# ScalarE takes a quarter of the first one-hot squares, all last stores leave from its queue, and a half tile of values is copied last

## The chip, the cores and the metric

The kernel runs on one core of one Trainium2 chip. A core has a matrix engine (TensorE, PE in the profile, with its weight loads shown as PEld), three engines for elementwise work (VectorE = DVE, ScalarE = ACT, GpSimd = POOL), a small engine that mostly issues transfers (SyncE = SP) and 16 DMA engines. Each engine works through its own list of instructions in order; they wait for each other with semaphores. The metric is the time of one execution on the device in microseconds (us), the median of several.

## The reference

Four batches of 1088 tokens go through an attention with polynomial features, and the result through a layer of 8 experts of which each token uses two.

```python
def phi(x):                       # x: (4, 4 heads, 1088, 32)
    a = np.einsum('rd,bhsd->bhsr', S1, x)
    b = np.einsum('rd,bhsd->bhsr', S2, x)
    return np.einsum('bhsi,bhsj->bhsij', a, b).reshape(*x.shape[:-1], r * r)
q_p, k_p = (phi(q), phi(k))
kv = np.einsum('bhsf,bhsd->bhfd', k_p, v)
z = np.sum(k_p, axis=2)
num = np.einsum('bhsf,bhfd->bhsd', q_p, kv)
den = np.einsum('bhsf,bhf->bhs', q_p, z)[..., None] + 1e-06
attn_out = (num / den).astype(np.float32)
x = np.ascontiguousarray(attn_out.transpose(0, 2, 1, 3)).reshape(B * S, H * D)   # (4352, 128)
...
logits = x @ w_gate
noise_scale = np.log1p(np.exp(x @ w_noise))
noisy_logits = logits + noise_scale * noise
top2 = np.argpartition(-noisy_logits, 2, axis=1)[:, :2]
top2_l = np.take_along_axis(noisy_logits, top2, axis=1)
top2_l = top2_l - top2_l.max(-1, keepdims=True)
top2_w = np.exp(top2_l)
top2_w /= top2_w.sum(-1, keepdims=True) + 1e-09
for e in range(E):
    for k in range(2):
        mask = top2[:, k] == e
        h = np.maximum(x[mask] @ w1[e], 0.0)   # 128 -> 1024
        out[mask] += top2_w[mask, k, None] * (h @ w2[e])
```

## The kernel before

**Stages.** The attention is done batch by batch (features L606 to L628, keys times values L669, queries L717 and L728). Then comes the routing of the tokens in steps `w`: router 0 takes the first four tiles of 128 tokens of the first batch, router 1 the other five of it, routers 2 to 4 the other batches. A router takes the logits, the two largest (L896 to L912), the mask `mk` of the chosen experts (L925, L927), counts by matmuls with triangles and ones how many tokens before a token chose the same expert (`counts`, L934 and L937), and from that a row in the memory `xs`, sorted by experts (L965 to L976). The gate weights `g` go through ScalarE (L906), GpSimd (L942), VectorE (L944) and GpSimd again (L945). The tokens times their weight (`xg`, L986) are scattered to `xs` by GpSimd's indirect DMAs, one for each tile and choice (L809).

**Blocks.** The experts work on blocks `u` of 128 or 256 rows of `xs`: fetch `xb`, turn it to `bT`, first matmuls to `hp` (L1094), relu to `h` on ScalarE (L1102), second matmuls to `acc` (L1109), copy to `y`, scatter to `pairs` (L809). Between these, TensorE does the attention of the next batch.

**The first four blocks** (`u < DIRECT = 4`) don't wait for scattered rows. For each of the four token tiles `c` a one-hot square `o` is made (L1040): row place against the token's position `pos`, times its gate `gm`. A matmul of the tokens with the square (`turn`, L1046) picks and turns the rows at once. `place` is a constant 128x128 tile; `pos` is made at L955 from the counts, `gm` at L961. VectorE makes these squares, except for the fourth of block 0, which GpSimd makes.

**Who sets the order.** Nothing of the order is written by hand. Every step is added as a `Job` with the engine, an estimated cost, what it reads and writes, and a priority (a lower number goes first). `Plan.order` is a list scheduler: at each step it takes those that could start within 0.3 us of the earliest, and of them the one of the lowest priority. For a TensorE job behind ScalarE's or VectorE's work it adds a margin `SLACK` = 0.5 us to the time at which the input is expected, once the plan is past 30 us (L105). For transfers, `margin` adds to the expected landing. The resulting lists are written once, so each number shifts places in all five lists. Where TensorE would idle in the plan before 28 us, it is given dummy matmuls on `zb` (L1421).

**The head's values.** The first batch's values come in as four full pieces and two small ones (`load_v`, L362). Copies make them to `vaug`: four full head copies and one for the half tile (L645), which stand with equal priority.

**The end.** Results are gathered from `pairs` (`pr`, issued by SyncE), added in twos (L1165), for the last batch's late pieces added to what TensorE computed (`bank`, L1172), and stored. `sums` (L1148) cycles through the queues it is given; the last call gives ("ACT", "SP", "SP") for the three pieces: the first store is issued by ScalarE, the others by SyncE. Then every engine loads `flag` (L1426) and branches past a fallback that serves an overflow of the blocks (L1428); SyncE waits for all transfers, and the engines close together (L1456).

Of the kernel before, what the change touches and what calls it, by code (L numbers as in the profile page):

```python
# [12 lines left out]
AF = mybir.ActivationFunctionType  # L13
# [16 lines left out]
class Job:  # L30
    def __init__(self, engines, cost, emit, lat, prio, size):
        self.engines, self.cost, self.emit, self.lat, self.prio, self.size = engines, cost, emit, lat, prio, size
        self.far, self.margin = False, 0.0
        self.paced = 0.0
        self.deps, self.opens, self.end, self.done = set(), [], None, None


class Plan:
# [17 lines left out]
    def new(self, tag):  # L56
        return Buf(tag)
# [30 lines left out]
    def order(self):  # L88
        free, done, moved, paced, lanes = {}, [], 0.0, [], []
        left = {j: len(j.deps) for j in self.jobs}  # L90
        after = {j: [] for j in self.jobs}
        for j in self.jobs:
            for d in j.deps:
                after[d].append(j)
        cand = [j for j in self.jobs if not left[j]]
        number = {j: i for i, j in enumerate(self.jobs)}

        def ready(j, e):

            at = 0.0  # L100
            for d in j.deps:
                if d.engine == e and d.size is None and not d.far:
                    at = max(at, d.end)
                elif e == "PE" and d.engine in ("ACT", "DVE") and d.done > self.HEAD:
                    at = max(at, d.done + self.SLACK)  # L105
                else:
                    at = max(at, d.done)
            return at

        while cand:  # L110
            starts = []
            for j in cand:
                at = 0.0
                for b in j.opens:
                    bufs, _, used = self.tags[b.tag]
                    if b.placed or len(used) < bufs:
                        continue
                    ends = [x.done for x in used[-bufs].users]
                    if None in ends:
                        at = None  # L120
                        break
                    at = max(at, max(ends))
                if at is None:
                    continue
                if j.size is not None:
                    if "SP" in j.engines:
                        at = max(at, moved - self.AHEAD)
                    if "POOL" not in j.engines and len(lanes) >= self.LANES:
                        at = max(at, lanes[-self.LANES])
                if j.paced and paced:  # L130
                    at = max(at, paced[-1] + j.paced)
                for e in j.engines:
                    starts.append((max(at, free.get(e, 0.0), ready(j, e)), j, e))
            assert starts, [(j.engines, j.prio, [b.tag for b in j.opens]) for j in cand]
            first = min(x[0] for x in starts)
            _, s, _, j, e = min((j.prio, s, number[j], j, e) for s, j, e in starts if s <= first + self.SOON)
            cand.remove(j)
            cost = j.cost[e] if isinstance(j.cost, dict) else j.cost
            j.start, j.end, j.engine = s, s + cost, e
            free[e] = j.end  # L140
            if j.paced:
                paced.append(s)
            j.done = j.end + j.lat + self.SYNC
            if j.size is not None:
                moved = max(moved, j.end + 0.6) + j.size / self.RATE
                j.done = max(j.done, moved + 0.8 if e == "SP" else j.end + 1.4 + 2 * j.size / self.RATE)
                if e != "POOL":
                    lanes.append(j.done)
                j.done += j.margin
            j.opens = [b for b in j.opens if not b.placed]  # L150
            for b in j.opens:
                b.placed = True
                self.tags[b.tag][2].append(b)
            done.append(j)
            for a in after[j]:
                left[a] -= 1
                if not left[a]:
                    cand.append(a)
        assert len(done) == len(self.jobs)
        return done  # L160
# [14 lines left out]
def kernel(  # L175
# [57 lines left out]
    def add(engines, cost, emit, **kw):  # L233

        if hold and engines in ("DVE", "PE"):
            kw["after"] = tuple(kw.get("after", ())) + tuple(hold)
        elif hold and engines == EV:
            engines = "ACT"
        return plan.add(engines, cost, emit, **kw)
# [3 lines left out]
    def tag(name, bufs, shape, dtype=F32, space=pool):  # L243
        plan.tag(name, bufs, lambda: space.tile(list(shape), dtype, name=name, tag=name, bufs=bufs))
# [48 lines left out]
    def vec(n):  # L293
        return 0.155 + 0.00104 * n

    def act(n):
        return 0.155 + 0.00086 * n
# [64 lines left out]
    def load_v(b, prio, queues=("SP",)):  # L362
        t = new("vld")
        vlds[b] = t
        src = v[b].rearrange("h (t n) d -> t h n d", n=TN)
        for l in range(4):
            dma(queues[l % len(queues)], lambda l=l: t.t[32 * l:32 * l + 32, :, 0:C, :].rearrange("p h c d -> p h (c d)"),
                lambda l=l: src[:, :, C * l:C * l + C, :].rearrange("t h c d -> t h (c d)"),
                (), [(t, l)], prio, size=131e3, issue=1.2, margin=MARGIN if b > 1 else 8.0 if b else VLATE)
        for l in range(2):  # L370
            dma(queues[l % len(queues)], lambda l=l: t.t[32 * l:32 * l + 32, :, C, :], lambda l=l: src[:, :, 32 + l, :],
                (), [(t, 4 + l)], prio, size=16e3, issue=0.6, margin=MARGIN if b > 1 else 8.0 if b else 0.0)

    w1s = const.tile([P, E, F], F32, name="w1s")
    w2s = const.tile([P, E, FJ, D], F32, name="w2s")
# [263 lines left out]
    def keys_values(b, prio, head=False, after=(), early=None):  # L639
        kT, qT, pk, pq, va = new("kT"), new("qT"), new("phk"), new("phq"), new("vaug")  # L640
        kld, qld, vld = klds[b], qlds[b], vlds[b]
        for h in range(H):
            add(("ACT", "POOL") if head else "ACT", {"ACT": act(256), "POOL": 0.4} if head else act(256), lambda e, h=h: copy(e, va.t[:, 0:C, h, 0:DH], vld.t[:, h, 0:C, :]),
                r=["ones_v"] + [(vld, l) for l in range(4)], w=[(va, h)], prio=prio + 2.2, after=hold)
        add("ACT", act(128), lambda e: A.copy(va.t[0:HB, C, :, 0:DH], vld.t[0:HB, :, C, :]),  # L645
            r=["ones_v", (vld, 4), (vld, 5)], w=[(va, H)], prio=prio + 2.2, after=hold)
        for i, (c0, c1) in enumerate(((0, 2), (2, 6), (6, 8)) if head else ((0, 4), (4, 8))):
            if early is not None and i == 0:
                turned(kT, kld, c0, c1, 22, True)
# [166 lines left out]
    def router(b, t0, n, w, x, lg, prio):  # L816
# [13 lines left out]
        def dve(cost, emit, r, w_, p=0, after=()):  # L830
            def step(e):
                ins = emit()
                if w == 0 and ins is not None:
                    marks.append((plan.now.end, ins))
            return add("DVE", cost, step, r=[B_.get(k, k) if isinstance(k, str) else k for k in r],
                w=[B_.get(k, k) if isinstance(k, str) else k for k in w_], prio=prio + p, after=after)
# [95 lines left out]
        def counts(e):  # L932
# [3 lines left out]
            for s in range(1, n + 1):  # L936
                T.matmul(ps.t[:, E * s:E * (n + 1)], lhsT=ones[:],  # L937
                         rhs=mk[:, 0:n + 1 - s, :].rearrange("p i e -> p (i e)"), start=False, stop=(s == n),
                         skip_group_check=True)
        add("PE", 0.06 * (n + 1), counts, lat=0.15, r=[B_["mk"], "earlier", "ones"], w=[ps], prio=prio)  # L940

        add("POOL", 0.25, lambda e: G.tensor_scalar(out=g1(), in0=g2(), scalar1=1.0, scalar2=1e-9, op0=ALU.add, op1=ALU.add),  # L942
            r=[(B_["g"], 1)], w=[(B_["g"], 0)], prio=prio - 0.5)
# [7 lines left out]
        if w == 0:  # L951

            pos, gm = new("pos"), new("gm")
            onehot.update(pos=pos, gm=gm, x=x)
            dve(q1, lambda: V.scalar_tensor_tensor(out=pos.t[:], in0=ps3()[:, 0:n, :], scalar=1.0, in1=t3("mk"),  # L955
                                                   op0=ALU.add, op1=ALU.mult), [ps, "mk"], [pos], -0.5)

            def gates():
                V.tensor_tensor(out=B_["f2"].t[:, :, 0:n, :], in0=B_["first"].t[:, :, 0:n, :],
                                in1=B_["g"].t[:, :, 0:n].unsqueeze(3).to_broadcast([P, 2, n, E]), op=ALU.mult)  # L960
                V.tensor_add(out=gm.t[:], in0=B_["f2"].t[:, 0, 0:n, :], in1=B_["f2"].t[:, 1, 0:n, :])  # L961
            dve(2 * q1, gates, ["first", "g"], ["f2", gm])

        def rows_of():
            V.tensor_tensor(out=t3("row"), in0=ps3()[:, 0:n, :], in1=pl.unsqueeze(1).to_broadcast([P, n, E]), op=ALU.add)  # L965
# [56 lines left out]

    tag("pos", 1, [P, 4, E])
    tag("gm", 1, [P, 4, E])


    TOP = -1000
# [2 lines left out]
    def block(u, w, e, r, n):  # L1030
# [5 lines left out]
        if u < DIRECT:  # L1036
            oh = new("o")
            for c in range(4):
                add(("POOL" if u == 0 and c == 3 else "DVE"), 0.85 if u == 0 and c == 3 else vec(64), lambda e_, c=c: (
                    G if e_ == "POOL" else V).tensor_scalar(  # L1040
                    out=oh.t[:, c, :], in0=place[:], scalar1=onehot["pos"].t[:, c, e:e + 1],
                    scalar2=onehot["gm"].t[:, c, e:e + 1], op0=ALU.is_equal, op1=ALU.mult),
                    r=["place", onehot["pos"], onehot["gm"]], w=[(oh, c)], prio=-900 if u == 0 else 12.5 + u)

            for c in range(4):
                gather = add("PE", mm(P), lambda _, c=c: T.matmul(  # L1046
# [353 lines left out]
        if w == 4:  # L1400
            sums(B - 1, part_of(B - 1, [(0, 4)]), w, 901)
    pieces = part_of(B - 1, [(4, 2), (6, 2)], True)
    sums(B - 1, [pieces[0], pieces[2], pieces[1]], NW, 902, ("ACT", "SP", "SP"))

    def idle(a, b):

# [54 lines left out]
```

## Time and profile before

| | us |
|---|---|
| median of 3 runs | 350.83 (350.19 to 351.37) |
| the profiled execution | 352.57 |
| its span in the profile | 350.6 |
| TensorE's clock in it | 0.993 of full |

Busy time of each engine in stretches of the span:

| stretch, us | PE | DVE | ACT | POOL |
|---|---|---|---|---|
| 0 to 25 | 22.81 | 18.75 | 9.01 | 18.14 |
| 25 to 34 | 8.15 | 8.32 | 2.66 | 6.15 |
| 34 to 82 | 46.46 | 34.43 | 20.60 | 36.90 |
| 82 to 134 | 51.11 | 32.99 | 19.62 | 41.34 |
| 134 to 343 | 208.65 | 52.55 | 81.02 | 131.79 |
| 343 to 350.5 | 0.06 | 0.42 | 0.00 | 0.00 |

In the profile a line of the timeline gives the start in us from the start of the span, the duration in us, the engine, the line of the kernel, the operation, output<-input by the program's names with shapes, how many instructions were merged (x4), and in brackets how long the engine was idle before and what it then waited for. An engine name with a q (SPq) stands for its sequencer: issues of transfers, semaphores, branches. The list of waits has the total in us, the number of times and the longest.

### The profile page before, as it was taken

Reading aid. Unit: us, or ns where it says so; the run is one execution under the profiler, and the core shown is the slowest. Engines: PE = TensorE matmul, PEld = TensorE weight load, DVE = VectorE, ACT = ScalarE, POOL = GpSimd, SP = SyncE. Lnnn points to the kernel's source line nnn. Section 1 sums busy time; section 2 is a strip of 40 time slices with the busy share of each in tenths; the row PEclk is TensorE's granted clock in tenths of the full one; section 3 lists DMA queues with packets and bytes.
Section 4 is the critical chain, followed back from the end, with each engine's and each line's share of the span. In section 5 each row is a group of like instructions: output and inputs, shape, how many; then the busy total and the mean of one; then the engine's idle time right before and its main releaser. Section 6 shows DMA issues by size and latency. Waiting matters only on the chain.

```text
span 350.6 us, 7490 instructions
## 1 busy us (share of the span) xinstructions
PE 337.2 (96%) x2586; PEld 314.1 (90%) x2586; DVE 147.5 (42%) x550; ACT 132.9 (38%) x297; POOL 234.3 (67%) x385
## 2 busy tenths in 40 slices
PE   8999999998999999999999999999999999999991
PEld 3858999998999988999999999999999999999990
DVE  6789894867536669556760001011101010212111
ACT  2343643442533344413434333433343334434330
POOL 8856759895999863988898988978334433454310
PEclk9999999999999999999999999999999999999997
DMA  7999849135571386411533213454126211115421
GB/s 201 351 348 258 267 121 310 40 77 147 133 215 40 70 188 126 121 47 31 93 60 70 60 40 60 78 178 104 39 36 185 63 32 29 26 32 177 134 71 39
DMA packets 68922, 41.17 MB, mean 117 GB/s; under 512 B 49877, under 2 KB 61078, under 8 KB 68880
## 3 DMA queue, kind: packets, MB, share of 16 engines
q1 hardware_dynamic: 63584, 31.09, 35.7%
q0 software_dynamic: 4704, 9.15, 7.9%
q10 hardware_dynamic: 592, 0.41, 0.5%
q8 instruction: 21, 0.34, 0.4%
q14 instruction: 21, 0.17, 0.2%
HBM read 24.18 MB, written 16.65 MB: 116 GB/s over the span
## 4 chain that ended last, share of the span: by engine, by line
PE 84%; DVE 5%; DMA 4%; POOL 2%; issue 1%; SPq 1%; ACT 1%; POOLq 0%; DVEq 0%
PE acc L1109 34%; PE hp L1094 33%; PE bank L606 4%; PE bank L728 4%; PE bank L669 4%; DMA kq<-in_k_dram 2%; PE bank L717 2%; POOL pairs L809 1%; DMA xb<-xs 1%; PE turn L1046 1%; PE bank L1241 1%; SPq L338 1%; DVE kT L590 1%; POOL zb L808 0%; DMA ix<-xs 0%
## 5 line engine op out<-in xcount | busy, mean ns | idle before, releaser
L1109 PEld LDWEIGHTS acc<-w2s,h 128*128 128x128 f32 x1152 | 146.0, 192 | 5.1 <-ACT h L1102 0.4
L1109 PE MATMUL acc<-w2s,h 128*128 128x128 f32 x1152 | 150.4, 275 | 0.0
L1094 PE MATMUL hp<-bT,w1s 128*128 128x128 f32 (+1 forms) x768 | 148.2, 328 | 0.2 <-ACT h L1102 0.2
L1102 ACT ACTIVATE h<-hp 128x512 f32<-128x512 f32 x144 | 85.9, 597 | 126.1 <-PE hp L1094 125.9
L1094 PEld LDWEIGHTS hp<-bT,w1s 128*128 128x128 f32 x768 | 111.7, 191 | 6.2 <-ACT h L1102 0.7
L809 POOL DMA_INDIRECT pairs<-y,ix x66 | 65.8, 997 | 64.2 <-ACT y L322 52.8
L809 POOL DMA_INDIRECT xs<-xg,to x72 | 74.3, 1031 | 20.2 <-issue 9.6
L808 POOL MEMSET zb<- 128x400 bf16 (+1 forms) x142 | 63.1, 444 | 0.2
L1082 DVE STREAM_TRANSPOSE bT<-xb 128x256 f32<-128x256 f32 (+1 forms) x40 | 15.6, 390 | 111.6 <-PE hp L1094 99.7
L322 ACT COPY y<-acc 128x128 f32<-128x128 f32 (+1 forms) x48 | 15.3, 319 | 27.2 <-PE acc L1109 24.7
L1165 DVE TENSOR_TENSOR o<-pr 128x512 f32<-128x512 f32 (+2 forms) x13 | 6.7, 525 | 37.5 <-DMA pr<-pairs 37.5
L728 PE MATMUL bank<-kvw,pT 128*128 128x98 f32 x144 | 18.2, 274 | 0.0
L728 PEld LDWEIGHTS bank<-kvw,pT 128*128 128x128 f32 x144 | 17.3, 192 | 0.5 <-DVE kvw L322 0.3
L669 PE MATMUL bank<-phk,vaug 128*128 128x128 f32 (+1 forms) x108 | 13.1, 277 | 0.0
L322 ACT COPY lo<-bank 128x256 f32<-128x256 f32 (+3 forms) x20 | 6.6, 328 | 16.8 <-PE bank L606 14.0
L669 PEld LDWEIGHTS bank<-phk,vaug 128*128 128x128 f32 (+1 forms) x108 | 12.5, 191 | 0.4
L322 ACT COPY pT<-bank 128x512 f32<-128x512 f32 (+1 forms) x16 | 8.8, 560 | 10.0 <-PE bank L717 8.0
L628 DVE TENSOR_TENSOR phk<-ab 128x512 f32<-128x512 f32 (+1 forms) x20 | 12.2, 631 | 0.4
L614 DVE TENSOR_TENSOR ab<-bank,lo 128x256 f32<-128x256 f32 (+3 forms) x20 | 7.2, 361 | 12.3 <-ACT lo L322 12.0
L628 DVE TENSOR_TENSOR phq<-ab 128x512 f32<-128x512 f32 (+1 forms) x20 | 11.9, 629 | 0.2
L986 DVE TENSOR_TENSOR xg<-x,g 128x512 f32<-128x512 f32 (+1 forms) x16 | 11.2, 748 | 0.0
L1421 PE MATMUL hp<-zb 128*128 128x512 bf16 x30 | 9.3, 442 | 1.7 <-DVE zb L439 1.3
(175 smaller groups left out, 240.6 us busy)
## 6 DMA issues: line engine op xcount, KB each, us to landing
xs<-pad SPq DMA_DIRECT2D x9, 516.0 KB
w1s<-in_moe_w_dram SPq DMA_DIRECT2D x8, 512.0 KB
w2s<-in_moe_w_dram SPq DMA_DIRECT2D x8, 512.0 KB
pr<-pairs SPq DMA_DIRECT2D x7, 512.0 KB
xb<-xs SPq DMA_DIRECT2D x96, 32.0 KB
kq<-in_k_dram SPq DMA_DIRECT2D x4, 544.0 KB
kq<-in_q_dram SPq DMA_DIRECT2D x4, 544.0 KB
vld<-in_v_dram SPq DMA_DIRECT2D x14, 128.0 KB
```

The lines of the kernel that those rows point to most:

```text
L322: paces.append(A.copy(o, i) if e == "ACT" else V.tensor_copy(o, i))
L606: T.matmul(ps.t[rows, 2 * W * i:2 * W * i + 2 * W], lhsT=lhsT, rhs=sk[:].rearrange("p c h x -> p (c h x)"), start=True, stop=True)
L628: V.tensor_tensor(out=jobs[i][2].t[rows, jobs[i][1]:jobs[m - 1][1] + 1, :, :].rearrange("p c h (i j) -> p (c h) i j", i=R), in0=factors(i, ...
L669: T.matmul(kvp.t[:, P * a:P * a + P], lhsT=va.t[0:K, t, hs, :].rearrange("p h d -> p (h d)"), rhs=pk.t[0:K, t, hs, :].rearrange("p h f -> ...
L728: T.matmul(ps2.t[:, c0:c0 + 2 * YW], lhsT=pT.t[:, P * (2 * i + a):P * (2 * i + a) + P], rhs=kvw.t[:, a, :], start=True, stop=True)
L808: G.memset(zb[:, 0:FIRST_SPACER if kind == "first" else SPACER], 0.0)
L809: ins = G.indirect_dma_start(**kw)
L986: V.tensor_tensor(out=xg.t[:, i, c0:c1, 0:D], in0=x.t[:, c0:c1, :], in1=B_["g"].t[:, i, c0:c1].unsqueeze(2).to_broadcast([P, c1 - c0, D]), ...
L1082: add("DVE", vec(P * n), lambda _: V.transpose(bT.t[:, 0:P * n], flat()), r=[xb], w=[bT], prio=TOP + u)
L1094: T.matmul(hp.t[:, P * n * i:P * n * (i + 1)], lhsT=w1s[:, e, P * (js * g + i):P * (js * g + i + 1)], rhs=bT.t[:, 0:P * n], start=True, st ...
L1102: paces.append(A.activation(out=h.t[:], in_=hp.t[:], func=AF.Relu))
L1109: T.matmul(acc.t[:, D * c:D * c + D], lhsT=h.t[:, P * (n * i + c):P * (n * i + c + 1)], rhs=w2s[:, e, j, :], start=(j == 0 and c == 0), st ...
```

## The change

Four things change; the rest of the file stays, and below L1040 lines stand 14 lower in the new file.

1. The square of tile `c = 3` of each of the first four blocks is made by ScalarE in two steps: the absolute value of `pos` minus `place`, then relu of `gm` minus `gm` times that. It is `gm` where place and position agree and 0 elsewhere, since both are whole numbers and `gm` is not negative. The negative of `gm` for that tile is a new tile `less`, made by GpSimd. The other three squares are VectorE's in all four blocks. The squares' priorities are now (-900, 12.9, 14.5, 15.5), where they were -900 and 12.5 + u.
2. The counts of routers 1 to 4 get a planning margin of 1.0 in place of 0.5.
3. The small transfers of the first values get a planning margin, and the copy of the half tile the priority 2.9 in place of 2.2 in the head.
4. The last three stores are all issued by ScalarE.

```diff
@@ class Job
-        self.far, self.margin = False, 0.0
+        self.far, self.margin, self.slack = False, 0.0, None
@@ Plan.order, ready
-                    at = max(at, d.done + self.SLACK)
+                    at = max(at, d.done + (self.SLACK if j.slack is None else j.slack))
@@ load_v
-                (), [(t, 4 + l)], prio, size=16e3, issue=0.6, margin=MARGIN if b > 1 else 8.0 if b else 0.0)
+                (), [(t, 4 + l)], prio, size=16e3, issue=0.6, margin=MARGIN if b > 1 else 8.0 if b else VLATE + 0.5)
@@ keys_values
-            r=["ones_v", (vld, 4), (vld, 5)], w=[(va, H)], prio=prio + 2.2, after=hold)
+            r=["ones_v", (vld, 4), (vld, 5)], w=[(va, H)], prio=prio + (2.9 if head else 2.2), after=hold)
@@ the router
-        add("PE", 0.06 * (n + 1), counts, lat=0.15, r=[B_["mk"], "earlier", "ones"], w=[ps], prio=prio)
+        counted = add("PE", 0.06 * (n + 1), counts, lat=0.15, r=[B_["mk"], "earlier", "ones"], w=[ps], prio=prio)
+        counted.slack = None if w == 0 else 1.0
...
+            less = new("less")
+            onehot["less"] = less
+            add("POOL", 0.25, lambda e: G.tensor_scalar(out=less.t[:], in0=gm.t[:, 3, :], scalar1=-1.0, scalar2=None, op0=ALU.mult),
+                r=[gm], w=[less], prio=prio - 0.5)
@@ block
-                add(("POOL" if u == 0 and c == 3 else "DVE"), 0.85 if u == 0 and c == 3 else vec(64), lambda e_, c=c: (
-                    G if e_ == "POOL" else V).tensor_scalar(
+                if c == 3:
+
+                    add("ACT", act(P), lambda e_, c=c: A.activation(
+                        out=oh.t[:, c, :], in_=place[:], func=AF.Abs, scale=-1.0, bias=onehot["pos"].t[:, c, e:e + 1]),
+                        r=["place", onehot["pos"]], w=[(oh, c)], prio=(-900, 12.9, 14.5, 15.5)[u])
+                    add("ACT", act(P), lambda e_, c=c: A.activation(
+                        out=oh.t[:, c, :], in_=oh.t[:, c, :], func=AF.Relu, scale=onehot["less"].t[:, e:e + 1],
+                        bias=onehot["gm"].t[:, c, e:e + 1]), r=[onehot["gm"], onehot["less"]], w=[(oh, c)], prio=(-900, 12.9, 14.5, 15.5)[u])
+                    continue
+                add("DVE", vec(P), lambda e_, c=c: V.tensor_scalar(
                     out=oh.t[:, c, :], in0=place[:], scalar1=onehot["pos"].t[:, c, e:e + 1],
                     scalar2=onehot["gm"].t[:, c, e:e + 1], op0=ALU.is_equal, op1=ALU.mult),
-                    r=["place", onehot["pos"], onehot["gm"]], w=[(oh, c)], prio=-900 if u == 0 else 12.5 + u)
+                    r=["place", onehot["pos"], onehot["gm"]], w=[(oh, c)], prio=(-900, 12.9, 14.5, 15.5)[u])
@@ the last call of sums
-    sums(B - 1, [pieces[0], pieces[2], pieces[1]], NW, 902, ("ACT", "SP", "SP"))
+    sums(B - 1, [pieces[0], pieces[2], pieces[1]], NW, 902, ("ACT",))
```

More of the change, by code (lines that the diff above doesn't have):

```diff
@@ L1024 @@
     tag("gm", 1, [P, 4, E])
+    tag("less", 1, [P, E])
     TOP = -1000
```

## The prediction, made before the changed kernel ran

> **What bounds the kernel now.** I read the page's busy shares first, then its slices, then the waits, the timeline at each remaining gap of TensorE (PE), and last what follows its last matmul.
>
> ```profile
> PE 337.2 (96%) x2586; PEld 314.1 (90%) x2586; DVE 147.5 (42%) x550; ACT 132.9 (38%) x297; POOL 234.3 (67%) x385
> PE   8999999998999999999999999999999999999991
> ```
>
> PE is the bound at full clock, so a change can win only where PE is idle or after it has ended. The stages show where: PE is busy 8.15 of 9.00 us in 25 to 34, 46.46 of 48 in 34 to 82, 51.11 of 52 in 82 to 134 and 208.65 of 209 in 134 to 343; then come 7.5 us without PE. So some 3.3 us of gaps lie between 25 and 134, nothing after, and 7.5 us at the end.
>
> The head (timeline 25 to 28), where the first block's four one-hot squares are made:
>
> ```profile
> 25.06 1.30 DVE L1040 TENSOR_SCALAR o<-place,pos,gm 128x128 f32<-128x128 f32 x3
> 25.13 0.87 POOL L1040 TENSOR_SCALAR o<-place,pos,gm 128x128 f32<-128x128 f32 x1 [0.80 <-DVE pos L955]
> ...
> 26.50 0.68 PE L1046 MATMUL turn<-o,x 128*128 128x128 f32 x4 [0.18 <-DVE row L965]
> ...
> 27.54 1.86 PEld L1094 LDWEIGHTS hp<-bT,w1s 128*128 128x128 f32 x16 [0.23 <-ACT bT L322]
> ```
>
> Third router (w=2): GpSimd (POOL) issues back to back until its gate step, VectorE (DVE) goes on from that, and PE's counts come last. The three groups are POOL's, DVE's and PE's timeline:
>
> ```profile
> 77.92 0.97 POOL L809 DMA_INDIRECT pairs<-y,ix  x1 [0.17 <-issue]
> 78.96 0.27 POOL L942 TENSOR_SCALAR g<-g 128x9 f32<-128x9 f32 x1
> ```
> ```profile
> 79.27 0.21 DVE L944 RECIPROCAL g<-g 128x9 f32<-128x9 f32 x1 [0.64 <-POOL g L942]
> 79.40 0.25 DVE L918 TENSOR_TENSOR first<-ids,pick 128x144 f32<-128x144 f32 x1
> 79.68 0.23 DVE L925 TENSOR_TENSOR mk<-first 128x72 bf16<-128x72 f32 x1
> ```
> ```profile
> 80.08 0.19 PE L934 MATMUL bank<-mk,earlier 128*128 128x72 bf16 x1 [1.34 <-DVE mk L927]
> ```
>
> PE stands 1.34 us there, and again at the fourth router:
>
> ```profile
> 131.72 0.19 PE L934 MATMUL bank<-mk,earlier 128*128 128x72 bf16 x1 [0.32 <-DVE mk L927]
> ...
> 132.46 1.72 PE L606 MATMUL bank<-sk,kT 128*128 128x128 f32 x13 [0.33 <-DVE kT L590]
> ```
>
> The end: stores, then SyncE (SP) reads the flag, branches over the fallback, and closes (the timeline, the two source lines, and SP's own waits: total, times, longest).
>
> ```profile
> 342.55 0.64 ACTq L338 DMA_DIRECT2D out_dram<-o  x1
> 342.77 1.77 SPq L338 DMA_DIRECT2D out_dram<-o  x2
> 343.10 0.42 DVE L1172 TENSOR_TENSOR o<-o,bank 128x256 f32<-128x256 f32 x1 [0.36 <-PE bank L1241]
> ```
> ```profile
> L1426 SPq TENSOR_LOAD <-flag x1: 979/979/979, 344.6 to 344.6; - x1
> ```
> ```profile
> L1428 SPq EVENT_SEMAPHORE  x8: 17/17/17, 348.1 to 348.7; - x8
> ```
> ```profile
> SPq L1428 <- SPq L1428: 2.5, 1, 2.5
> ```
>
> SP's flag load starts only after its second store (342.77 + 1.77); its branch is at 345.6, and 2.5 us pass before its next instruction, which waits for nothing. The DMA view of that time shows 8 KB packets of the instruction queue, so I read it as a fetch past the skipped body. The last store has landed by 346.48: SP is later than the data.
>
> **What the Trainium skill says.** "ScalarE: Activation LUTs", Table sets: relu and abs are in every table set, so the new functions should not reload one; the trace has a single ACT_TABLE_LOAD (L514), and the changed program keeps one. The same page, What ACT_TABLE_LOAD costs, prices an ACTIVATE with a pointer bias at 280 + 0.833 N ns and another pointer at 93 more; the 128x512 h took 597 ns at L1102 and 128x32 ones with a pointer follow each other in 0.19 us here. "GPSIMD Engine Reference", Specifications: POOL and DVE share an SBUF interface; the trace agrees, since a DVE square takes 0.43 us beside POOL's square and 0.29 alone (x4 in 1.17 at 29.30). "DMA: Bandwidth & Descriptors", Anatomy of one DMA: some 2.0 us fixed, mostly the receipt; the last store took 1.95 from the end of its issue (344.53) to landing.
>
> **The change part by part.** The order of the built programs shows that the list planner moves instructions on all engines up to about 180 us; the work of PE stays the same.
>
> *One-hot squares.* POOL's 0.87 and three later DVE squares go; ScalarE (ACT) gets 4 pairs, POOL one 128x8 operation (0.20, as L945). A pair is an estimate: 0.54 (two spacings of 0.27, the 128x128 copy) to 0.87 (0.387 + 0.480 by the skill). I take 0.75. POOL's new operation is hidden: gm is there at 24.81, so it ends near 25.1, and the first Relu asks for it only after its Abs, near 25.4; without that cover it would cost its 0.2. DVE now makes six squares in a row, undisturbed: the third at 25.06 + 3 x 0.29 = 25.93 in place of 26.36; ACT's first pair ends at about 25.85. But on ACT two pairs and the lo copy (0.35) stand before bT: 25.07 + 1.5 + 0.35 = 26.9, against 27.22. So the first hp comes 0.3 earlier (0 to 0.5). The second block's turn now stands ahead of the first block's acc, which removes its wait of 0.63 + 0.36 and part of the 0.55 before: with the first 0.3 about 1.6 us of PE. This is early arrival at the next wait only.
>
> The price: router 0's rows on DVE now wait for six squares and for the later lo copy: 26.23 becomes about 27.2, and the first scatter moves from 28.48 by the same 1.0. POOL issues scatters without a gap from there to 41.95, so the delay runs on; two of them took 2.12 and 1.47 in place of 0.97[...], and 2.77 us idle stand before 51.71. I carry d = 0.8 (0 to 1.2) to the next router.
>
> *Counts' slack.* The margin has no instruction of its own; it puts more PE work ahead of the counts of routers 1 to 3. Summing PE's instructions in both orders at the trace's times (0.2232 us each for 128 columns in fp32) gives 49.67 before and 52.35 after at w=2: 2.68 us more work in front. The counts' input is later too: DVE's reciprocal, which waits for POOL, now stands ahead of five index searches (5 x 0.16 = 0.8), and POOL is late by d. PE would arrive at 78.74 + 2.68 - 1.6 = 79.8, and the input is there at 80.9 + d: PE still waits, and the gain past w=2 is 2.68 - 0.8 - d = 1.9 - d. At w=3 1.76 us more work stands in front, and DVE's gate work comes before a transpose that waited 2.21 us for its fetch at 128.15, so the mask is ready at about 130.9 + d in place of 131.67; the waits of 0.32 + 0.33 and some 0.15 of drain go: 0.8. Sum 2.7 - d = 1.9. One POOL pair more ahead of the scatters of w=2 and w=3 hides in POOL's idle time (1.65 before 85.27; about 4 near 135). After 134 PE has no gap, so what is gained by then stays.
>
> *Half tile of values last.* ACT's copies for the head (L645) change places. Whatever comes earlier meets DVE's kT at 17.26, which waits for the keys' transfer landing at 17.24: 0 (-0.1 to 0.1).
>
> *Stores.* Three on ACT: 342.55 + 0.64 + 0.59 + 0.64 to 0.98 (SP's own took 0.587 and 0.984) gives 344.4 to 344.8 for the end of issue, 344.53 before. SP's last work is now the loads ending at 338.02, so its flag load, branch and 2.5 us lie beside PE work and are over by 341.7. ACT reads the flag after 344.7: its load took 0.907 and its step from branch to semaphore 0.5, which gives 346.2, before the last landing at 344.7 + 1.95 = 346.65. From SP's last store semaphore to the end is 350.55 - 348.60 = 1.95; end 348.6 instead of 350.55: 1.9 us (1.6 to 2.3). If ACT suffers the 2.5 us fetch as well, its semaphore is at 348.2, and the gain is 0.5 or nothing.
>
> **Sum.** 1.9 + 1.9 = 3.8 us. Span 350.6 becomes 346.8, the profiled execution 352.57 (2.0 outside the span) 348.8. That execution lies 1.7 above the median of the plain runs, so I take the difference off the median: 350.83 - 3.8 = 347.0.
>
> **Rivals.**
> A, forecast: both gains, 346.0 to 348.2.
> B, only one of the two. PE loses its part if d is above 1.2 or a reordered wait takes its place (any of the gaps of 0.36 to 0.45 at 76.69 and 108.46 may grow): 350.83 - 1.9 = 348.9. Or ACT inherits SP's fetch: 348.7. For: the fetch is seen on SP alone, and I only infer why; ACT's branch passed in 0.5.
> C, neither: 350.0 to 351.4. Both defects of B at once, or the change does not do what it says because the planner's new order leaves the input of the counts as late as the work put before it (at d = 1.9 the 0.8 and d have eaten the 2.68, and only the fourth router's 0.8 is left).
> D, slower: router 0's scatters are pushed by 1.0 into the weight loads (rings busy until 38) and the first block's rows, whose landing took about 4 us at 46.72, come late for PE. The price is d less 2.7, less the tail; it decides from d = 4.6 with the tail gained, or 2.7 without. At d = 6: 350.83 + 3.3 - 1.9 = 352.2. For: POOL's chain has no slack from 28 to 42 and from 52 to 79. Against: nothing in it multiplies 1.0 into 5.
>
> **How the numbers follow.** A 0.52, B 0.28, C 0.09, D 0.11. The predicted time is A's, 347.0. The range 345.8 to 350.2 takes A with the low ends of d and of the pair (2.7 + 2.3 off), all of B and a corner of C; C's rest and D are left out. 0.3% is 1.05 us, about what a measurement of this kernel can tell from no change: A and B lie beyond it, so faster 0.80, same 0.10, slower 0.10 (a corner of D counts as same).
>
> **What would show it.** Right: the first scatter near 29.4; PE's wait before the third counts about 1.0 to 1.5, none before the fourth; PE's last matmul near 341.2; SP's flag load near 338; the last SP semaphores 1.9 us before the end with landing just ahead. Wrong: an ACT branch with 2.5 us behind it; the pair of 51.71 later by more than 1.2; a second table load; a new PE wait of 0.5 or more between 34 and 134.

## The result and the profile after

| | before | changed |
|---|---|---|
| median of 6 runs, us | 350.46 (349.43 to 351.37) | 346.94 (346.26 to 347.57) |
| profiled execution, us | 352.57 | 347.08 |
| its span, us | 350.6 | 345.1 |
| TensorE's clock in it | 0.993 | 0.994 |

The ratio is 0.9901 with an interval of 0.9877 to 0.9925: 3.5 us faster, between 2.6 and 4.3. The two profiled executions lie 5.5 us apart; the 2 us between this and the medians are explained below, by a second profile of the kernel before.

The page of the changed kernel, busy shares and slices of TensorE (PE):

```profile
PE 336.2 (97%) x2585; PEld 313.9 (91%) x2586; DVE 146.4 (42%) x547; ACT 136.4 (40%) x305; POOL 232.1 (67%) x385
PE   8999999999999999999999999999999999999992
```

The 8 that stood in the slice from 79 us on is a 9 now. By stretches, PE is busy 8.46 of 9.00 us in 25 to 34 (8.15 before), 48.00 of 48 in 34 to 82 (46.46) and 51.76 of 52 in 82 to 134 (51.11).

The head of the changed kernel, lines of the timeline of all engines:

```profile
25.13 1.62 DVE L1054 TENSOR_SCALAR o<-place,pos,gm 128x128 f32<-128x128 f32 x6
25.18 0.40 ACT L1047 ACTIVATE o<-place,pos 128x128 f32<-128x128 f32 x1 [0.19 <-DVE pos L956]
...
25.68 0.49 ACT L1050 ACTIVATE o<-o,gm,less 128x128 f32<-128x128 f32 x1
26.08 0.39 ACT L1047 ACTIVATE o<-place,pos 128x128 f32<-128x128 f32 x1
...
26.90 0.35 ACT L322 COPY lo<-acc 128x256 f32<-128x256 f32 x1
27.15 0.27 ACT L322 COPY bT<-turn 128x128 f32<-128x128 f32 x1
...
27.47 2.05 PE L1108 MATMUL hp<-bT,w1s 128*128 128x128 f32 x16 [0.24 <-ACT bT L322]
...
29.88 1.38 POOL L809 DMA_INDIRECT xs<-xg,to  x1 [4.14 <-DVE xg L991]
```

Six squares take VectorE (DVE) 1.62 us, 0.27 each. ScalarE's (ACT) pair starts at 25.18 and the next at 26.08: 0.90 a pair, 0.50 from the start of the first step to that of the second and 0.40 from there to the next pair. The copies `lo` and `bT` stand behind two pairs, so `bT` comes at 27.15, 0.07 earlier than before on the clock of the span. Since everything lies 0.07 later in this execution (`pos` at 24.90, 24.83 before), the first `hp` gained 0.14 us. The first scatter (29.88) lies 1.4 us later than before (28.48).

The third router (w=2) in the changed kernel; timelines of POOL, of DVE and of PE:

```profile
77.03 0.97 POOL L809 DMA_INDIRECT pairs<-y,ix  x1 [0.17 <-ACT g L906]
78.07 0.28 POOL L943 TENSOR_SCALAR g<-g 128x9 f32<-128x9 f32 x1
```
```profile
78.38 0.21 DVE L945 RECIPROCAL g<-g 128x9 f32<-128x9 f32 x1 [1.01 <-POOL g L943]
...
79.61 0.23 DVE L925 TENSOR_TENSOR mk<-first 128x72 bf16<-128x72 f32 x1
```
```profile
79.17 1.06 PE L1123 MATMUL acc<-w2s,h 128*128 128x128 f32 x8
80.06 0.20 PE L934 MATMUL bank<-mk,earlier 128*128 128x72 bf16 x1
...
130.12 0.20 PE L934 MATMUL bank<-mk,earlier 128*128 128x72 bf16 x1
...
130.39 2.03 PE L606 MATMUL bank<-sk,kT 128*128 128x128 f32 x16
```

No wait is left in front of the counts, at 80.06 (1.34 before) or at 130.12 (0.32 before and 0.33 behind it). The input comes as late as before (79.96, 80.03 before), and PE, which stood waiting before, now comes only then: it has 474 matmul records behind it since its first `turn` (the counts' own left out, here and below), where it had 450.

The end: the timeline, the lines of the flag load and of the branch, and SyncE's (SP) waits:

```profile
338.70 3.04 ACTq L338 DMA_DIRECT2D out_dram<-o  x3
339.25 0.42 DVE L1186 TENSOR_TENSOR o<-o,bank 128x256 f32<-128x256 f32 x1 [0.36 <-PE bank L1255]
```
```profile
L1440 SPq TENSOR_LOAD <-flag x1: 741/741/741, 334.2 to 334.2; - x1
```
```profile
L1442 SPq EVENT_SEMAPHORE  x8: 17/17/17, 337.8 to 343.4; - x8
...
L1442 SPq COMPARE_BRANCH  x1: 45/45/45, 335.0 to 335.0; - x1
```
```profile
SPq L1442 <- SPq L1442: 8.0, 4, 3.7
```

SP's branch falls at 335.0, before the last sums. Its 2.7 us to the next instruction (337.8) lie beside PE's work. After that its semaphores are real waits for the stores, which landed at 341.70, 342.49 and 343.27; SP passed the last of them at 343.29. From the end of VectorE's last sum to the end of the span it is 5.38 us, 7.03 before.

### The profile page after: what moved, and what is told of

Same layout as the page of the kernel before. It is cut to its first block, busy times and chain, and to the rows that moved or that the text cites. A ratio compares the mean times of both kernels' runs of the same rounds, so it can differ in the third digit from the quotient of the medians.

```text
span 345.1 us, 7493 instructions
## 1 busy us (share of the span) xinstructions
PE 336.2 (97%) x2585; PEld 313.9 (91%) x2586; DVE 146.4 (42%) x547; ACT 136.4 (40%) x305; POOL 232.1 (67%) x385
## 4 chain that ended last, share of the span: by engine, by line
PE 95%; DVE 2%; ACT 1%; issue 1%; POOL 0%; DVEq 0%; ACTq 0%; POOLq 0%
PE acc L1123 37%; PE hp L1108 37%; PE bank L606 5%; PE bank L728 4%; PE bank L669 4%; PE bank L717 2%; PE hp L1435 1%; PE acc L669 1%; PE bank L1255 1%; PE turn L1060 1%; PE bank L690 0%; ACT o L1050 0%; PE bank L937 0%; DVE lg L747 0%; ACT o L1047 0%
## 5 line engine op out<-in xcount | busy, mean ns | idle before, releaser
L809 POOL DMA_INDIRECT pairs<-y,ix x66 | 65.1, 986 | 66.1 <-ACT y L322 55.9
L809 POOL DMA_INDIRECT xs<-xg,to x72 | 73.0, 1014 | 19.2 <-issue 9.1
L669 PEld LDWEIGHTS bank<-phk,vaug 128*128 128x128 f32 (+1 forms) x108 | 12.5, 191 | 0.4
L614 DVE TENSOR_TENSOR ab<-bank,lo 128x256 f32<-128x256 f32 (+3 forms) x20 | 7.2, 360 | 12.5 <-ACT lo L322 12.4
```

The lines of the kernel that those rows point to most:

```text
L669: T.matmul(kvp.t[:, P * a:P * a + P], lhsT=va.t[0:K, t, hs, :].rearrange("p h d -> p (h d)"), rhs=pk.t[0:K, t, hs, :].rearrange("p h f -> ...
L809: ins = G.indirect_dma_start(**kw)
```

## The experiments

All ratios are to the kernel before, with 95% intervals. "PE" is the time from its first `turn` to the end of its last matmul, "end" from the end of VectorE's last sum to the end of the span, each in the run's one profile. The kernels were timed in four sessions, each with the kernel before beside it: the changed kernel; then the edits alone; then the edits undone; then the last four rows. A difference between ratios of two sessions carries both intervals.

| kernel | ratio | PE, us | end, us |
|---|---|---|---|
| before | 1 | 317.5 | 7.03 |
| before, second profile | one time, 351.19 us | 315.7 | 7.22 |
| only the stores | 0.9938 (0.9920 to 0.9956) | 315.7 | 5.07 |
| only the margin | 0.9999 (0.9985 to 1.0014) | 315.7 | 7.12 |
| only the squares | 0.9976 (0.9960 to 0.9991) | 316.1 | 7.10 |
| changed | 0.9901 (0.9877 to 0.9925) | 313.6 | 5.38 |
| changed without the stores | 0.9946 (0.9926 to 0.9967) | 313.7 | 7.17 |
| changed without the margin | 0.9939 (0.9923 to 0.9954) | 315.2 | 4.76 |
| changed without the squares | 0.9955 (0.9937 to 0.9972) | 316.8 | 5.02 |
| changed without the half tile's place | 0.9881 (0.9861 to 0.9900) | 313.8 | 4.92 |
| middle store on SP | 0.9901 (0.9867 to 0.9936) | 313.6 | 5.83 |
| router 0's rows first | 0.9912 (0.9890 to 0.9934) | 317.6 | 5.06 |
| four squares on VectorE | 0.9908 (0.9872 to 0.9944) | 316.9 | 5.61 |
| margin 1.5 | 0.9920 (0.9889 to 0.9952) | 314.7 | 4.86 |

### The kernel before, once more

No edit.

> The kernel before, unchanged, profiled a second time. In the first profile GpSimd's first scatter to pairs waited until 51.71 because the transfer first_at landed 4.2 us after its issue. Theory: that is chance (the rows' own landing decides when SyncE starts its weight loads), so the chain's start moves by about 1 us from run to run: 50.5 to 51.7 here, with PE's wait before the third router's counts between 0.3 and 1.4 us. Rival: it is fixed by the order, then 51.7 and 1.3 again. The time: 349.4 to 351.4.

The timeline of this second profile, POOL's and then PE's:

```profile
50.22 1.66 POOL L809 DMA_INDIRECT pairs<-y,first_at  x1 [0.74 <-DVE at L975]
...
77.67 0.28 POOL L942 TENSOR_SCALAR g<-g 128x9 f32<-128x9 f32 x1
```
```profile
78.80 0.19 PE L934 MATMUL bank<-mk,earlier 128*128 128x72 bf16 x1 [0.18 <-DVE mk L927]
```

The same program started its first scatter to `pairs` 1.5 us earlier and PE waited 0.18 us in place of 1.34. The kernel with only the stores changed, whose lists are the same up to the end, is a third sample: 0.13 us there, and PE's stretch is 315.7 again. So chance made most of the wait on which the prediction leaned. In the first profile the transfer `first_at`, issued at 46.72, had landed only at 50.91, and POOL's instruction that waits for it passed at 50.94. In the second profile it was issued at 46.47 and had landed at 48.86. It lands in sixteen parts, and only the last of them was late: it came 1.90 us behind the fifteenth in the first profile, 0.16 in the second and 0.03 to 1.08 in the other twelve. Why stays open. The start of SP's weight loads doesn't tell the two apart: they started at 48.58 in the first profile and at 48.34 in the second, before the landing in both.

The times of the kernel before scatter accordingly. In the last session its 26 executions fall into two groups of 13, from 349.05 to 350.63 and from 351.69 to 352.96, and the median of 351.16 lies between them, where no execution is. No trace was kept that says whether `first_at` makes the two groups; the ratios of the last four rows rest on that median.

### The last stores, alone and undone

```diff
-    sums(B - 1, [pieces[0], pieces[2], pieces[1]], NW, 902, ("ACT", "SP", "SP"))
+    sums(B - 1, [pieces[0], pieces[2], pieces[1]], NW, 902, ("ACT",))
```

Alone, in the kernel before:

> The kernel before with only the three last stores on ScalarE; all else, and so every list up to the end, as before. Theory: the end gains 1.6 us (from VectorE's last sum to the end of the span 5.85 us in place of 7.45), ratio 0.9953. Rival: in the changed kernel the end was shorter because other things had moved, then 0 here, ratio 1.000. SyncE's flag load must stand 8 to 10 us before the end, and 1.7 us from the last landing to the end.

Undone, in the changed kernel:

> The changed kernel with the last stores back on ScalarE, SyncE, SyncE. Theory: it loses the end's gain and keeps TensorE's: 1.6 to 2.2 us slower than the changed kernel, ratio to the kernel before 0.9945 to 0.9965, and from VectorE's last sum to the end of the span 7.0 to 7.2 us in place of 5.4. Rival (the end's gain needs nothing of this part): ratio 0.990.

Alone it gained 2.2 us (1.5 to 2.8), and the end became 5.07 us; counted from the start of the sum, as the expectation does, 5.49. SP's flag load stood 10.5 us before the end, a little more than expected. Undone it lost 1.6 us against the changed kernel (across two sessions), and the end was 7.17 again. The end's gain is the stores' part and nothing else's: PE's stretch doesn't move with it (315.7 alone, 313.7 undone). In the kernel with the stores back on SP, its branch line and its waits:

```profile
L1442 SPq EVENT_SEMAPHORE  x8: 17/17/17, 344.5 to 345.0; - x8
...
L1442 SPq COMPARE_BRANCH  x1: 45/45/45, 342.0 to 342.0; - x1
```
```profile
SPq L1442 <- SPq L1442: 2.5, 1, 2.5
```

The branch at 342.0, nothing for 2.5 us, then eight semaphores in a row: none of them waited, as in the kernel before.

### The middle store on SyncE

```diff
-    sums(B - 1, [pieces[0], pieces[2], pieces[1]], NW, 902, ("ACT",))
+    sums(B - 1, [pieces[0], pieces[2], pieces[1]], NW, 902, ("ACT", "SP", "ACT"))
```

> The changed kernel with the middle one of the three last stores on SyncE again (ScalarE, SyncE, ScalarE). Theory (SyncE's flag load, branch and the 2.5 us after it are what the end gained by): SyncE's branch falls some 1.9 us behind VectorE's first last sum, its first semaphore 2.5 us later, so the end is again SyncE's: 5.5 to 6.0 us from VectorE's last sum to the end of the span against 4.8 to 5.4, 0.2 to 0.8 us slower than the changed kernel. Rival (the landing of the last store sets the end): ScalarE's third issue comes 0.6 us earlier, so 0.3 to 0.6 us faster than the changed kernel, 4.4 to 4.8 us of end.

The orders of PE, DVE and POOL are those of the changed kernel. The time can't tell theory and rival apart (0.9901, interval 0.9867 to 0.9936). The branch line and SP's waits can:

```profile
L1442 SPq EVENT_SEMAPHORE  x8: 17/17/17, 343.0 to 343.5; - x8
...
L1442 SPq COMPARE_BRANCH  x1: 45/45/45, 340.4 to 340.4; - x1
```
```profile
SPq L1442 <- SPq L1442: 2.6, 1, 2.6
```

One store on SP is enough to bring its branch back behind the last sum and its eight unwaited semaphores back to the end, though the last store had landed at 342.05, 1.0 us ahead of the first of them: 5.83 us, where the eight kernels with three stores on ACT end in 4.76 to 5.61. It had been expected at 5.5 to 6.0. The rival, that the last landing alone sets the end, would have shown 4.4 to 4.8; here 3.2 us pass from the last landing to the end, where the changed kernel has 1.8. With 5.61 in one of the eight, the figure 5.83 alone would prove little; the order of branch, landing and semaphores does.

### The margin and the squares, each alone

The margin:

```diff
+        counted.slack = None if w == 0 else 1.0
```

> The kernel before with only the counts' planning margin of 1.0. Theory (both parts serve one wait): more PE work stands ahead of the third and fourth counts, so PE's waits of 1.34 and of 0.32 + 0.33 us go, 1.3 to 2.0 us, ratio 0.9943 to 0.996. Rival (the one-hot change brings it): no more than 0.3 us, ratio above 0.999.

The squares (the diff of `block` and the tile `less`):

> The kernel before with only the first four blocks' fourth squares on ScalarE and the new priorities. Theory: PE's gaps from 25 to 34 shrink by 0.3 to 1.6 us but the third counts' input comes no earlier, so PE only waits longer there: 0 +- 0.5 us, ratio 0.9986 to 1.0014, first scatter 1.4 us later (near 29.9). Rival: the head's gain stays to the end: 1.0 to 1.6 us, ratio 0.9955 to 0.997.

A line of PE's timeline with only the margin, then two with only the squares:

```profile
105.39 0.66 PE L717 MATMUL bank<-ident,phq 128*128 128x128 f32 x4 [0.68 <-ACT pT L322]
```
```profile
80.63 0.19 PE L934 MATMUL bank<-mk,earlier 128*128 128x72 bf16 x1 [0.63 <-DVE mk L927]
...
105.50 0.66 PE L717 MATMUL bank<-ident,phq 128*128 128x128 f32 x4 [0.68 <-ACT pT L322]
```

The margin alone is worth nothing: 0.9999, as the rival had it. Its list holds 482 records ahead of the third counts, where 450 stood before, and PE has no wait there; but then it waits 0.68 us at 105.39 for a copy (L717) and 0.32 at 123.66. The squares alone gave 0.8 us, between what theory and rival expected (interval 0.3 to 1.4 us), so this run decides for neither. Their list, with the margin still at 0.5, holds 474 records ahead of the third counts, and PE waits there all the same. So either edit puts more work ahead of the counts, and neither brings TensorE's gain by that: PE's stretch is 315.7 and 316.1, where the second profile of before has 315.7.

### The margin and the squares, each undone

> The changed kernel with the counts' margin back at 0.5. Theory (the margin is worth something only with the earlier squares): a wait of 0.4 to 1.3 us comes back before the third counts and others of 0.3 to 0.7 behind it, 0.7 to 1.5 us slower than the changed kernel, ratio 0.992 to 0.9945. Rival (the margin is worth nothing in any company, as it was alone): ratio 0.990 +- 0.001.

> The changed kernel with all squares on VectorE (one on GpSimd) and the old priorities. Theory: stores and margin alone give no more than the stores do, ratio 0.9938 +- 0.001, PE's gaps from 25 to 34 are those of before. Rival (margin with the half tile's place is what brings TensorE's part): 0.990 to 0.991.

Without the margin, POOL's, DVE's and PE's lines of the timeline at the third router, and later one at a transpose:

```profile
79.20 0.27 POOL L943 TENSOR_SCALAR g<-g 128x9 f32<-128x9 f32 x1
...
80.66 0.19 PE L934 MATMUL bank<-mk,earlier 128*128 128x72 bf16 x1 [0.62 <-DVE mk L927]
```
```profile
105.53 0.66 PE L717 MATMUL bank<-ident,phq 128*128 128x128 f32 x4 [0.68 <-ACT pT L322]
```

Both kernels have 474 records ahead of the third counts. The one without the margin has its gate step on POOL 1.1 us later (79.20 for 78.07), because the planner placed the first scatter to `pairs` behind all ten row scatters (at 68.42 in place of 50.57), so POOL's row of 17 indirect DMAs up to that step starts at 51.64 in place of 50.57. The squares alone have the same order (68.39 and 51.62). PE waits 0.62 there and 0.68 at L717, where the changed kernel has 0 and, at 107.61, 0.24. That makes 1.06 us of the 1.6 by which PE's stretches differ (315.2 and 313.6), and it is all of the difference in PE's idle time (1.88 and 0.83 in the whole stretch); the rest lies in time that the profile counts as busy, and the trace doesn't say more of it. The ratio agrees: 0.9939 against 0.9901, 1.3 us.

Without the squares the head's gaps are those of before (0.31, 0.18, 0.36), and PE waits 0.58 at the third counts, 0.68 at L717, 0.31 at 124.69: 316.8, worse than the margin or the squares alone, and the whole kernel 0.9955, not the 0.9938 that I had expected. TensorE's gain of 2.1 us (315.7 to 313.6) belongs to the pair of margin and squares. Taken singly they are worth 0 and 0.8 by time. The medians of the kernels with one edit undone, timed side by side, say the same: with the half tile's place undone, which costs nothing (below), 346.79 us, and without stores, margin or squares 349.01, 348.89 and 349.66, 2.1 to 2.9 more.

### The half tile's place

```diff
-                (), [(t, 4 + l)], prio, size=16e3, issue=0.6, margin=MARGIN if b > 1 else 8.0 if b else VLATE + 0.5)
+                (), [(t, 4 + l)], prio, size=16e3, issue=0.6, margin=MARGIN if b > 1 else 8.0 if b else 0.0)
...
-            r=["ones_v", (vld, 4), (vld, 5)], w=[(va, H)], prio=prio + (2.9 if head else 2.2), after=hold)
+            r=["ones_v", (vld, 4), (vld, 5)], w=[(va, H)], prio=prio + 2.2, after=hold)
```

> The changed kernel with the half tile of values copied in the old place. Theory: the head waits at its keys' transfer near 17.2 us either way, so nothing changes, ratio 0.990 +- 0.001. Rival (the copy's place frees ScalarE early and starts everything earlier): ratio 0.991 to 0.9925 with the first turn 0.3 to 0.8 us later.

0.9881, with an interval that overlaps the changed kernel's: putting the copy back cost nothing. The first `turn` stood at 25.43, 25.62 in the changed kernel, so nothing started earlier through the new place.

### Router 0's rows before the second block's squares

```diff
-                        r=["place", onehot["pos"]], w=[(oh, c)], prio=(-900, 12.9, 14.5, 15.5)[u])
+                        r=["place", onehot["pos"]], w=[(oh, c)], prio=(-900, 13.2, 14.5, 15.5)[u])
```
(the same in the other two places)

> The changed kernel with the second block's squares at priority 13.2 in place of 12.9, so that VectorE does three squares, then router 0's rows and weights, then the other nine. The work of TensorE ahead of each counts is the same. Theory (later scatters cost the time by which the third counts' input comes later): first scatter 0.5 to 0.9 us earlier than 29.9, the input of the third counts 0.2 to 0.6 earlier; TensorE has arrived there without a wait in the changed kernel, so no more than 0.2 us is won, and the second block's turn loses some: ratio 0.989 to 0.993. Rival (the delay of the scatters runs on to the end): 0.5 us faster than the changed kernel, ratio 0.987 or less.

The first scatter came at 28.94, 0.94 us earlier (0.68 counted from the first `turn`), the third counts' input 0.43 earlier (79.53), and nothing was gained: 0.9912. The second block's `turn` waits 0.35 us again (at 32.35, 0.36 before). PE's stretch of 317.6 isn't to be compared: in this profile the granted clock fell to 0.93 between 110 and 134 us, by the table of stretches, and the median of its runs says 347.8.

### All four squares on VectorE, in the new order

The two ACTIVATEs and `less` are taken out, and VectorE makes `c = 3` too, with the new priorities.

> The changed kernel with all four squares of each of the first four blocks on VectorE, at the new priorities, and without the tile less. Theory (it is the order, not ScalarE, that brings TensorE's part): VectorE does eight squares in a row, the first scatter comes 0.4 to 0.6 us later than 29.9, the first hp 0.1 to 0.3 later; the rest stays, ratio 0.990 to 0.992. Rival (ScalarE's help is needed): 0.7 us or more slower than the changed kernel, ratio 0.993 or more.

Lines of its timeline:

```profile
25.12 2.15 DVE L1040 TENSOR_SCALAR o<-place,pos,gm 128x128 f32<-128x128 f32 x8
...
27.22 1.86 PEld L1094 LDWEIGHTS hp<-bT,w1s 128*128 128x128 f32 x16 [0.23 <-ACT bT L322]
...
29.76 1.38 POOL L809 DMA_INDIRECT xs<-xg,to  x1 [4.03 <-DVE xg L987]
...
80.38 0.19 PE L934 MATMUL bank<-mk,earlier 128*128 128x72 bf16 x1 [0.44 <-DVE mk L927]
...
107.03 0.66 PE L717 MATMUL bank<-ident,phq 128*128 128x128 f32 x4 [0.68 <-ACT pT L322]
```

The ratio is that of the theory (0.9908), but its interval, 0.9872 to 0.9944, takes in the rival's 0.993 too. In the head the details went the other way than expected: eight squares on VectorE take 0.53 us more than six, but ACT has no pairs in front of `lo` and `bT`, so the first `hp` comes at 27.22 in place of 27.47 and the first scatter at 29.76, not later than with ScalarE's help. So the order of the squares is enough for the head's gain. Further on "the rest stays" did not hold: PE waits 0.44 us at the third counts and 0.68 at L717, where the changed kernel waits 0 and, at L690, 0.24. Whether that comes of the missing ScalarE or of the list that the planner made without it, and whether ScalarE's quarter is of use, stays open. By the medians of its session it took 348.10, the kernel with the middle store on SP 347.43. (The clock fell to 0.95 between 110 and 134 in this profile, so its 316.9 isn't compared either.)

### A margin of 1.5

```diff
-        counted.slack = None if w == 0 else 1.0
+        counted.slack = None if w == 0 else 1.5
```

> The changed kernel with the counts' margin at 1.5. TensorE's list then holds 0.9 us more work ahead of the third counts and 0.9 us less ahead of the fourth. Theory (the margin is worth what waits it covers; at 1.0 none is left at the third counts): no gain, 0 to 0.5 us slower because the routers' results come later, ratio 0.990 to 0.992. Rival (more margin is always better): 0.988 or less.

0.9920: no gain. The wait at L717 is back (0.68 us at 106.42), with one of 0.21 at 75.34. It came in six of the seven kernels here in which the margin or the squares are missing or altered, whatever the edit. So TensorE's gain looks tied to the one list that the changed numbers give, and no run shows it to grow with the margin. No kernel of this study beats the changed one by more than the intervals allow to tell; the one with the half tile in its old place is as good.

## Why the prediction was right, point by point

**The sum.** 3.8 us were forecast, 3.5 measured by the medians; 347.0 and 346.94. Of its two halves the end was right as worked out. TensorE's came out at the right size through steps of which several were wrong, so that its size is luck.

**The end: right.** 1.9 us (1.6 to 2.3) was forecast, and 1.65 in the two profiles, 2.2 alone and 1.6 undone by time were found. The cause was as stated: SP's flag load, its branch and the 2.5 us after it left the path (the branch at 335.0), the last landing took their place (343.27, then 1.8 us to the end), and ACT passed its own branch in 0.5 us (342.8 to 343.3). The term that was mis-sized is ACT's issue of three stores: 1.87 to 2.21 us in the sum, 3.04 (with the gaps between) in the profile, because one issue took 1.50. In the seven other kernels with these stores the second or third took 1.01 to 1.61.

**The squares: the price was too low.** A pair was taken at 0.75 with bounds 0.54 to 0.87; it is 0.90, about the sum of its durations of 0.40 and 0.49. The two prices that I quoted from "ScalarE: Activation LUTs", What ACT_TABLE_LOAD costs (0.387 and 0.480), are right to some 0.01 us; the error was to shade their sum towards the spacing of the copies, although the second step reads what the first writes: it starts 0.10 after the first has ended. The first `hp` therefore gained 0.14, not 0.3. The head's 1.6 us was too high: up to the second counts the time that PE spent beyond its records since its first `turn` fell from 2.0 to 1.1 us (180 records in 22.04 us before, 188 in 22.11 after, at the 0.1116 of one record), so 0.8. The sum had mixed engines. Two lines from before, at the second block's `turn`:

```profile
32.37 0.27 ACT L322 COPY bT<-turn 128x128 f32<-128x128 f32 x1 [0.63 <-PE turn L1046]
...
32.69 0.49 PE L1046 MATMUL turn<-o,x 128*128 128x128 f32 x2 [0.36 <-ACT bT L322]
```

The 0.63 is ScalarE's idle time and the 0.55 that of the weight loads (PEld); only 0.36 is PE's, and all its idle time from 25 to 34 was 0.85 by the table of stretches.

**The delay d: wrong for the trace that I argued from.** The first scatter moved by 1.4 (forecast 1.0). But POOL's gate step at the third router came 0.9 earlier than in the first profile, d = -0.9 where 0.8 (0 to 1.2) was carried. Against the second profile of before it came 0.4 later, which is nearer to what the order sets, though chance sits in that profile too; the rest goes with the late landing of `first_at`. Two things took the delay up on the way: the scatters themselves (0.5 of it was left at the eighth, 41.48 against 40.98) and the wait for their landing (the fetch `xb` at 44.41, 44.53 before).

**The margin: it got the credit for what took both edits.** "It puts more PE work ahead of the counts" was worked out as 2.68 us by comparing the orders before and after, and put down to the margin. The 24 records were there (474 for 450), but either edit moves work there, the squares alone 24 records and the margin alone 32, and in the changed kernel taking the margin back leaves 474. What the margin adds beside the squares is at POOL, whose gate step comes 1.1 us earlier, at the fourth counts (892 records ahead for 868 without it) and at the transposes of L717. A comparison of two orders that differ by four edits says what moved, not which edit moved it.

**The wait at the third counts.** PE was to wait there still, 1.0 to 1.5 us, and waits 0. Its arrival was forecast at 79.8 and was 80.06; the input at 80.9 + 0.8, and it was 79.96. The reciprocal placed ahead of the index searches cost what was said: from POOL's gate step to the end of the mask 1.07 us before and 1.89 now, so 0.82. The gain of the fourth router (0.8) came as 0.5.

**TensorE's part in all.** Forecast 1.9; the profiles give 3.9 against the first profile of before and 2.1 against the second. The medians (3.5 less the end's 1.6 to 2.2, so 1.3 to 1.9; and 1.9, between 1.2 and 2.6, for the changed kernel without the stores) agree with the second. PE's last matmul ended at 339.21, not near 341.2. The first profile held a wait of 1.34 us that two other profiles of the same list don't have, and the forecast drew part of its 1.9 from that wait. What the change took away against the second profile is smaller idle time in three places (busy 47.81 of 48 and 51.35 of 52 there, 48.00 and 51.76 now, and 0.31 more from 25 to 34): 0.9 of the 2.1 us. The other 1.2 is time that the profile counts as busy, for 2438 matmul records in both, and stays unexplained. Asking whether the wait was typical would have been better.

**The rest.** The half tile was worth nothing, as said. No second table load came. Rival B's two defects (ACT's own fetch, a new wait in PE's place) didn't come; the new wait did come in every kernel that had only one of margin and squares, 0.68 at L717. Rival D needed a d of 4.6, and it was -0.9 or 0.4.

## What to carry to other kernels

After the last matmul, look at which engine's closing instructions come last: one whose sequencer must still read a flag and branch can be relieved by giving its last transfers to another queue, and that was about half of the gain here. Where a planner writes the order, try edits singly and undone before crediting one of them, because two that were worth 0 and 0.8 us alone were worth about 2 together. Profile the kernel before twice before leaning on a wait of a microsecond that a DMA's landing starts.

## What the hardware showed that had not been expected

- SP's branch over the skipped body cost 2.5 to 3.2 us until its next instruction in all fourteen profiles, where ACT's branch to the same place took 0.5 or less, DVE's 0.6 and POOL's 0.2. Three 8 KB packets of an instruction queue lie around it in the first profile of before. That it is a fetch was inferred, and why SP alone pays so much was not tried.
- The issue of one of the three last stores took 0.55 to 0.70 us or 1.0 to 1.6. In thirteen of the fourteen profiles there is one long issue, and it is each time the one that began within 0.5 us after the start of a 16 KB packet on the other instruction queue (0.96 to 1.36 us long). With the middle store on SP no issue began during that packet, and none was long. That they share something is likely; no run separates them.
- Squares of 128x128 in fp32 took VectorE 0.27 us each in rows of six and eight, and 0.43 on average in the row of three beside GpSimd's square.
